# Two attention and token-MLP layers on one core: the weight search moved one block ahead, and PSUM divided once into one-bank tiles

## The chip, the core and the metric

The kernel runs on one core of one Trainium2 chip. A core has a matrix engine (TensorE: PE in the profile, its weight loads PEld), a vector engine (DVE), a scalar engine (ACT), a general engine (POOL), and a queue for DMA issues (SyncE: SP). Matmuls write PSUM, which is divided into eight banks of 128 x 512 fp32 numbers. The metric is the device time of one execution in microseconds (us). The kernel before takes 1268.96 us, the median of three runs from 1268.88 to 1269.1 us.

## The reference

Two layers, each an attention block `A` and an MLP over tokens `B`, with the same weights in both layers. S = 2048 tokens, D = 1024 channels, 32 heads, F = 3584.

```python
def _A_ref(x, wqkv, wo):            # x: (1, 2048, 1024)
    qkv = (x @ wqkv) ...            # 32 heads of 32
    idx = pos[:, None] - arange(8) * 2      # 8 keys, every second token back
    logits = where(idx >= 0, (q . k[idx]) * 32 ** -0.5, -1e9)
    o = softmax(logits) . v[idx]
    return o.reshape(B, S, D) @ wo

def _B_ref(x, w1, b1, w2, b2):
    h = _layernorm(x)
    u = gelu(einsum("bsd,sf->bdf", h, w1) + b1)     # mixes tokens
    return (einsum("bdf,fs->bds", u, w2) + b2).transpose(0, 2, 1)

for _ in range(2):
    x = x + _A_ref(_layernorm(x), wqkv, wo)
    x = x + _B_ref(_layernorm(x), w1, b1, w2, b2)
```

## The kernel before

Tokens are split by parity (`c` = 0, 1: the dilation is 2), so that a query's eight keys are neighbours; each half has eight tiles of 128 tokens. Each layer has these stages in order of time.

1. **Values.** In layer 0 `start_up` normalizes x and multiplies it with the value columns. `V_` (L300) writes a two-bank PSUM tile for each of 16 token tiles, and `E_` (L308, L309) copies both banks to bf16 with one ACT instruction of 128 x 1024. Layer 1 uses `v_proj` with one-bank tiles (L393, L395).
2. **Attention.** 32 visits, two for each of 16 pairs of head group and parity. PE runs per visit: `scores` of this visit (L439), `values` of the visit before (L470 to L487), and two chunks of the query or key projection of the next pair (`qk_chunk`, L408: 8 matmuls each). ACT runs: two copies out of the chunks (L412 or L415), one exponential over a two-bank score tile (L442, 128 x 640), and a logarithm and an exponential for the division (L490, L491). DVE multiplies the exponentials with a band mask (`mask`, L454, four instructions), and divides (L493).
3. **Output projection.** `out_proj`: for each of 16 token tiles two halves of eight matmuls (L523), each followed on DVE by an addition out of PSUM (`add`, L530), and by layer norm pieces (L541, L545, L549) in an order that `chain_` fixes.
4. **First MLP product**, `gemm1`: F is cut into 14 blocks of 256. Block 0 is multiplied plainly (`plain`, L603). Blocks 1 to 13 use a Winograd form of Strassen's scheme: the 2 x 2 blocks of w1 (parity by half of the 256 columns) and of h take 7 products of eight matmuls each (`product`, L700) where a plain product takes 8. I call them P1 to P7, in the order of the code: P1 a(0,0).B11 into `pa`; P2 S0.T0 into `pd`; P3 S1.T1 added to `pb`; P4 a(1,0).B21 added to `pa`; P5 S2.T2 added to `pc`; P6 S3.B22 added to `pb`; P7 a(1,1).T3 added to `pc`; a(c,l) is the part of w1 of parity c and half l of the columns. S0 to S3 are sums of weights (`weight_sum`, DVE, L617), T0 to T3 sums of h (`token_sums`, POOL, L617, made once).
5. **Second MLP product**, `gemm2`: 16 token tiles of two halves, 28 matmuls each (L807), with an addition out of PSUM on DVE (L809).

For P2 to P7 the weights are fp16, and so that no sum overflows, each block of w1 is scaled by a power of two found from its greatest absolute value. That is **the weight search**, in layer 0 alone (layer 1 reads the sums back from DRAM, `load_sums`). For block `far`:

- `top` (L666): two DVE reductions over the two 128 x 2048 weight tiles, one number for each partition;
- `share` (L670, L672): SP writes these 128 x 2 numbers to DRAM (`mxd<-mx`) and, when that has landed, reads them back to all partitions (`bc<-mxd`);
- `power` (L638 to L643): five small DVE instructions make the factor `cs` and its inverse `ci`;
- `scale_w` (L676): ACT scales the two weight tiles, and `weight_sum` makes S0 to S3.

The factors of blocks 1 and 2 are made during attention (`pre_load`, `pre_top`). In block `fb` of the loop the search of `far = fb + 2` stands beside the scaling of `nxt = fb + 1`:

```python
if first and more:
    if nxt > NPRE:
        chain_(V, power, nxt, nxt + 1, bc_[nxt][:])
    chain_(A, scale_w, nxt, 0)
if seek:
    for c in range(DIL):
        chain_(V, top, far, c)
    share(far)
```

Each engine takes its instructions in order. `in_order` fixes the order on PE, and `chain_(V, ...)`, `chain_(A, ...)` that on DVE and ACT. DVE's order in block fb is therefore: power(fb+1), top(fb+2) twice, the addition that makes Y after P5, S0 of block fb+1, the addition that makes Z after P6, S1 to S3 of block fb+1. ACT's order is: `move(pb, pa)` after P1 (L709), `scale_w(fb+1, 0)`, `move(Z, pd)` after P2, `move(pc, pb)` after P3, gelu of `pa`, `scale_w(fb+1, 1)`, three gelus (L715). P5 adds onto what `move(pc, pb)` wrote.

Weights come through a pool of nine tiles of 512 KB (`wp`). A load waits until the tile that it takes over has had its last reader. SP's order is the planner's: it issues the loads of w1 for block fb+4 early in block fb, around the write of that block's sums (`sd<-Sw`, L692), and then the two transfers of `share`.

**PSUM** has three divisions. `psum_pools(m=2, s=2, a=1)` gives two one-bank tiles `m` and three two-bank tiles (`s` twice, `acc`). At the second output tile after the visits, the division becomes eight one-bank tiles `m`, until `gemm1` ends, and then the first one again. Every such switch waits until the tiles of the old division are free.

Of the kernel before, what the change touches and what calls it, by code (L numbers as in the profile page):

```python
# [9 lines left out]
ACT = mybir.ActivationFunctionType  # L10
ALU = mybir.AluOpType
# [6 lines left out]
P = 128  # L18
H = 32
DH = 32  # L20
W = 8
# [7 lines left out]
def kernel(  # L29
# [57 lines left out]
    ps = {}  # L87

    def psum_pools(**bufs):
        if ps:  # L90
            ps.pop("stack").close()
            ps.clear()
        ps["stack"] = ExitStack()
        for n, b in bufs.items():
            ps[n] = ps["stack"].enter_context(tc.tile_pool(name=f"ps{n}", bufs=b, space=bass.MemoryType.PSUM))

    ctx.callback(psum_pools)

    def m_tile():
        return ps["m"].tile([P, 512], FP32, name="m", tag="m")  # L100

    def s_tile():
        return ps["s"].tile([P, 2, 512], FP32, name="s", tag="s")

    def a_tile():
        return ps["a"].tile([P, 2, 512], FP32, name="acc", tag="acc")

    def pair(k):

        k %= 4  # L110
        if k == 3:
            ms = [m_tile(), m_tile()]
            return [m[:] for m in ms], None
        t = a_tile() if k == 1 else s_tile()
        return [t[:, n, :] for n in range(2)], t
# [123 lines left out]
    def start_up(v, wv):  # L239
# [45 lines left out]
        def tr(k, hf):  # L285
            tps[k, hf] = ps["m"].tile([P, KD // 2, P], BF16, name="m", tag="m")
            for j in range(KD // 2):
                lo = (hf * KD // 2 + j) * P
                r = nc.tensor.transpose(tps[k, hf][:, j, :], (xc[k] if k < 2 else xs[k])[:, lo:lo + P], ident[:])
            return r  # L290
# [5 lines left out]
        def V_(k, n, kts):  # L296
            if k not in pss_:
                pss_[k] = a_tile() if k % 3 == 1 else s_tile()
            for kt in kts:
                r = nc.tensor.matmul(pss_[k][:, n, :], lhsT=hT[:, kt, cols(*order[k])], rhs=wv[kt // 2][:, kt % 2, n * 512:(n + 1) * 512],  # L300
                                     start=(kt == 0), stop=(kt == KD - 1))
            return r

        def E_(k):
            c, i = order[k]
            dst, src = v[c][i][:].rearrange("p (n d) -> p n d", n=NDC), pss_[k][:]
            if k < 2:
                return nc.scalar.activation(out=dst, in_=src, func=ACT.Identity, scale=rss[k])  # L308
            return nc.scalar.copy(out=dst, in_=src)  # L309
# [4 lines left out]
        wm = s_tile()  # L314

        def W_(n):
            for _ in range(n):
                r = nc.tensor.matmul(wm[:, 0, :].rearrange("p (n q) -> p n q", q=P), lhsT=warm[:],
                                     rhs=warm[:].unsqueeze(1).to_broadcast([P, 4, P]), start=True, stop=True)
            return r  # L320
# [109 lines left out]
    def scores(u, b):  # L430
        q, k = qB[u % 2], kT[u % 2]
        s0 = (2 * u + b) % NS * HB
        ss = s_tile()
        for i in range(HB):
            lo = (b * HB + i) * P
            for r in range(P // KG):
                rp = slice(r * KG, (r + 1) * KG)
                dst = ss[rp, i // 2, i % 2 * HG * GW:(i % 2 + 1) * HG * GW].rearrange("p (h k) -> p h k", k=GW)
                mm = nc.tensor.matmul(dst, lhsT=k[:, lo + r * KG:lo + (r + 1) * KG],  # L439
                                      rhs=q[:, :, lo + r * KG:lo + r * KG + GW], start=True, stop=True)  # L440
        pc = pcp.tile([P, HB, HG, GW], BF16, name="pc", tag="pc")
        nc.scalar.activation(out=pc[:].rearrange("p (n t) h k -> p n (t h k)", n=2), in_=ss[:, :, 0:2 * HG * GW],  # L442
                             func=ACT.Exp, scale=scale, bias=shift[:])
        exps[:] = pc, s0
        return mm
# [12 lines left out]
    def values(u, b, v, oT):  # L458
        g, c = divmod(u, DIL)
        acc = a_tile()  # L460
# [3 lines left out]
        for i in range(-1 if b else 0, HB):  # L464
            t = t0 + i
            for h in range(HG):
                hp = slice(h * DH, (h + 1) * DH)
                lhs = v[c][t][:, g * P + h * DH:g * P + (h + 1) * DH]
                if i < 0:
                    nc.tensor.matmul(acc[hp, 0, 0:W], lhsT=lhs, rhs=Pm[:, h, sp, P:KW], start=True, stop=False,  # L470
                                     skip_group_check=True)
                else:
                    w = KW if i < HB - 1 else P
                    nc.tensor.matmul(acc[hp, 0, i * P:i * P + w], lhsT=lhs, rhs=Pm[:, h, s0 + i, 0:w],  # L474
                                     start=(t == 0), stop=(i == HB - 1), skip_group_check=True)
        for h in range(HG):
            hp = slice(h * DH, (h + 1) * DH)
            nc.tensor.matmul(acc[hp, 1, :].rearrange("p (t q) -> p t q", q=P), lhsT=ones[:], rhs=Pm[:, h, s0:s0 + HB, 0:P],
                             start=True, stop=False, skip_group_check=True)
# [3 lines left out]
        for lo_, n_, t_ in runs:  # L483
            for h in range(HG):
                hp = slice(h * DH, (h + 1) * DH)
                dst = acc[hp, 1, :].rearrange("p (t q) -> p t q", q=P)[:, t_:t_ + n_, 0:W]
                mm = nc.tensor.matmul(dst, lhsT=ones[:], rhs=Pm[:, h, lo_:lo_ + n_, P:KW], start=False, stop=True,  # L487
                                      skip_group_check=True)
        rd = x2("rd", [P, 512], FP32)
        nc.scalar.activation(out=rd[:], in_=acc[:, 1, :], func=ACT.Ln)  # L490
        nc.scalar.activation(out=rd[:], in_=rd[:], func=ACT.Exp, scale=-1.0)  # L491
        lo = c * SC + t0 * P
        norm.append(lambda: nc.vector.tensor_tensor(out=oT[g][:, lo:lo + HB * P], in0=acc[:, 0, :], in1=rd[:], op=ALU.mult))  # L493
# [99 lines left out]
    def plain(fb, h2, g):  # L593
# [3 lines left out]
        for fl in range(GF):  # L597
            pairs.append([m_tile()[:] for _ in range(NDC)])
# [48 lines left out]
    def gemm1(h2, g, first):  # L647
# [80 lines left out]
        if first:  # L728
            load_w1(2)
            last[A] = normed[0]  # L730
# [7 lines left out]
        load_w1(3)  # L738

        for fb in range(1, NFB):  # L740
            nxt, far = fb + 1, fb + 2
# [3 lines left out]
            pa, pd, pb, pc = (m_tile()[:] for _ in range(4))  # L745
# [8 lines left out]
            if first and more:  # L754
                if nxt > NPRE:
                    chain_(V, power, nxt, nxt + 1, bc_[nxt][:])
                chain_(A, scale_w, nxt, 0)
# [7 lines left out]
            if fb + 3 < NFB:  # L765
                load_w1(fb + 3)
# [8 lines left out]
            if first and more:  # L775
                chain_(V, weight_sum, nc.vector, nxt, 0)
            in_order(product, pb, Ss[fb][:, 3], B22, False)
# [18 lines left out]
    def gemm2(c, i, w2t, g, src, dst, to_hT):  # L796
# [3 lines left out]
        aps, _ = pair(i * DIL + c)  # L800
        parts = [(0, 512, aps[0]), (512, 512, aps[1])]
        final = not to_hT and (c, i) == order[-1]
        if final:
            parts[1:] = [(512, 384, aps[1][:, 0:384]), (896, 128, s_tile()[:, 0, 0:128])]
# [16 lines left out]
    psum_pools(m=2, s=2, a=1)  # L821
    hT, qB = new_hT(), new_qB()
    for li in range(2):
# [77 lines left out]
        for k, (c, i) in enumerate(order[4:]):  # L901
            if k == 1:
                psum_pools(m=8)
# [16 lines left out]
        psum_pools(m=2, s=2, a=1)  # L920
# [39 lines left out]
```

## Time and profile before

| | |
|---|---|
| median of three runs | 1268.96 us |
| the profiled execution, as timed | 1269.96 us |
| its span, first to last instruction | 1268.2 us |
| PE busy | 1233.4 us (97%) |
| DVE / ACT / POOL busy | 565.5 / 484.3 / 75.3 us |
| P1 to P7 of blocks 1 to 13, layer 0 | 275.32 to 449.94 us of the span |
| the same in layer 1 | 913.40 to 1070.53 us |
| one matmul of 128 x 512 after another | 0.216 us |

A row of a timeline has the start and the length in us, the engine, the line, the operation, what it writes and reads, and, where the engine was idle before, for how long and what ended that. PE's matmuls overlap: a row gives 0.38 us for one, but the next begins 0.216 us after it, so that an idle time shown for PE is about 0.16 us shorter than the time lost. Idle time of an engine that is not the bound costs nothing.

### The profile page before, as it was taken

How to read it: one execution, taken by the hardware profiler on the slowest of the kernel's cores; microseconds unless marked ns; L12 is line 12 of the kernel's file. 1: busy time of each engine (PE TensorE's matmuls, PEld its weight loads, DVE VectorE, ACT ScalarE, POOL GpSimd, SP SyncE). 2: the span in 40 equal slices, each digit the busy share in tenths (PEclk: the TensorE clock that was granted, in tenths of full speed). 3: DMA queues.
4: the chain of work that ended last, by engine and by line, in shares of the span. 5: the costliest groups of instructions: out<-in, count | busy, mean ns of one | idle time of the engine just before them, and what ended most of it. 6: DMA issues, size and time to landing. Idle time of an engine off the chain costs nothing.

```text
span 1268.2 us, 19616 instructions
## 1 busy us (share of the span) xinstructions
PE 1233.4 (97%) x8066; PEld 571.8 (45%) x8214; DVE 565.5 (45%) x1073; ACT 484.3 (38%) x755; POOL 75.3 (6%) x79
## 2 busy tenths in 40 slices
PE   9999999999989899999999999999999999999998
PEld 4444444444434444444444444444444444444444
DVE  7467777866676423223210577778411111111111
ACT  5366664476566510000023566645543433000000
POOL 0000000460000000000000000003800000000000
PEclk9999999999999999999999999999999999999999
DMA  8812224755665636457510112246655643335330
GB/s 243 132 50 78 68 83 127 207 161 158 172 179 139 180 87 174 115 133 174 129 50 1 44 50 51 81 168 197 176 153 179 184 143 119 92 108 161 97 94 34
DMA packets 215465, 157.55 MB, mean 124 GB/s; under 512 B 46672, under 2 KB 191824, under 8 KB 212048
## 3 DMA queue, kind: packets, MB, share of 16 engines
q1 hardware_dynamic: 215376, 156.30, 44.6%
q8 instruction: 64, 1.05, 0.4%
q14 instruction: 25, 0.20, 0.1%
HBM read 113.78 MB, written 30.42 MB: 114 GB/s over the span
## 4 chain that ended last, share of the span: by engine, by line
PE 85%; DMA 8%; DVE 5%; issue 1%; ACT 0%; ACTq 0%; SPq 0%
PE m L408 17%; PE s L807 15%; PE m L700 14%; PE m L523 8%; PE acc L807 8%; PE m L807 7%; PE m L393 4%; DMA bc<-mxd 4%; DVE mx L666 4%; PE s L300 3%; DMA mxd<-mx 3%; PE m L603 2%; PE s L439 2%; PE acc L300 1%; PE acc L474 1%
## 5 line engine op out<-in xcount | busy, mean ns | idle before, releaser
L807 PEld LDWEIGHTS <-w 128*128 128x128 bf16 x1820 | 177.0, 98 | 212.2 <-issue 2.3
L408 PE MATMUL m<-hT,wqk 128*128 128x512 bf16 x963 | 223.5, 379 | 6.3 <-issue 4.6
L807 PE MATMUL s<-g,w 128*128 128x512 bf16 (+1 forms) x902 | 199.8, 374 | 2.8 <-ACT g L715 1.7
L700 PE MATMUL m<-T,Sw 128*128 128x512 f16 x624 | 144.7, 382 | 14.3 <-ACT m L709 14.3
L408 PEld LDWEIGHTS <-wqk 128*128 128x128 bf16 x1024 | 95.3, 98 | 117.9 <-issue 10.7
L454 DVE TENSOR_TENSOR Pm<-pc,band 32x640 bf16<-32x640 bf16 x256 | 123.5, 483 | 53.0 <-ACT pc L442 46.4
L700 PEld LDWEIGHTS <-Sw 128*128 128x128 f16 x832 | 81.6, 98 | 115.4 <-issue 19.3
L523 PE MATMUL m<-wo,oT 128*128 128x512 bf16 x500 | 110.9, 379 | 2.9 <-DVE xn L530 2.0
L209 ACT ACTIVATE ln<-mv,eps 128x1 f32<-128x1 f32 x64 | 18.9, 295 | 232.1 <-DVE mv L217 186.2
L807 PE MATMUL acc<-g,w 128*128 128x512 bf16 x442 | 100.3, 379 | 0.4
L700 PE MATMUL m<-h,w 128*128 128x512 bf16 x416 | 98.3, 379 | 0.0
L807 PE MATMUL m<-g,w 128*128 128x512 bf16 (+1 forms) x441 | 97.4, 376 | 0.4
L809 DVE SCALAR_TENSOR_TENSOR xo<-s,b_sb,xs 128x512 bf16<-128x512 f32 (+1 forms) x33 | 24.4, 739 | 161.8 <-PE s L807 135.3
L700 PEld LDWEIGHTS <-w 128*128 128x128 f16 (+1 forms) x624 | 61.0, 98 | 73.6
L617 DVE TENSOR_TENSOR py<-pz,m 128x512 f32<-128x512 f32 x26 | 17.9, 688 | 149.4 <-PE m L700 111.4
L419 DVE COPY qB<-qs 32x512 bf16<-32x512 bf16 x136 | 38.1, 280 | 91.4 <-ACT qs L415 89.9
L523 PEld LDWEIGHTS <-oT 128*128 128x128 bf16 x512 | 49.4, 98 | 62.9 <-DVE xn L530 3.0
L617 POOL TENSOR_TENSOR T<-h 128x512 f16<-128x512 bf16 x16 | 18.5, 1154 | 832.2 <-DMA xr<-xb 581.0
L676 ACT ACTIVATE w<-w,cs 128x2048 f16<-128x2048 bf16 x26 | 51.8, 1998 | 30.1 <-DVE cs L643 30.1
L442 ACT ACTIVATE pc<-s,shift 128x640 bf16<-128x640 f32 x64 | 51.2, 800 | 13.3 <-PE s L439 13.3
L415 ACT CAST qs<-m 128x512 bf16<-128x512 f32 x64 | 37.5, 586 | 48.3 <-PE m L408 48.3
L393 PE MATMUL m<-wv,hT 128*128 128x512 bf16 x251 | 55.2, 379 | 0.3
(95 smaller groups left out, 1187.8 us busy)
## 6 DMA issues: line engine op xcount, KB each, us to landing
w<-in_B_w_dram SPq DMA_DIRECT2D x60, 512.0 KB, 5.8
w<-in_B_w_dram SPq DMA_DIRECT2D x64, 448.0 KB, 4.8
sd<-Sw SPq DMA_DIRECT2D x13, 1024.0 KB, 7.1
Sw<-sd SPq DMA_DIRECT2D x13, 1024.0 KB, 4.9
wqk<-in_A_wqkv_dram SPq DMA_DIRECT2D x16, 512.0 KB, 5.0
xa<-xn SPq DMA_DIRECT2D x32, 256.0 KB, 2.3
xs<-xa SPq DMA_DIRECT2D x32, 256.0 KB, 3.3
wo<-in_A_wo_dram SPq DMA_DIRECT2D x8, 512.0 KB, 5.4
```

The source lines that it names most:

```text
L300: r = nc.tensor.matmul(pss_[k][:, n, :], lhsT=hT[:, kt, cols(*order[k])], rhs=wv[kt // 2][:, kt % 2, n * 512:(n + 1) * 512], start=(kt == ...
L393: nc.tensor.matmul(ps[:], lhsT=hT[:, kt, cols(c, i)], rhs=wv[kt // 2][:, kt % 2, n * 512:(n + 1) * 512], start=(kt == 0), stop=(kt == KD - 1))
L408: mm = nc.tensor.matmul(ps[:], lhsT=wts[part][:, kt, (g % 2) * P:(g % 2 + 1) * P], rhs=hT[:, kt, lo:lo + 512], start=(kt == 0), stop=(kt = ...
L415: nc.scalar.copy(out=qs[:], in_=ps[:])
L419: nc.vector.tensor_copy(out=qB[u % 2][hp, h, ls], in_=qs[hp, :])
L442: nc.scalar.activation(out=pc[:].rearrange("p (n t) h k -> p n (t h k)", n=2), in_=ss[:, :, 0:2 * HG * GW], func=ACT.Exp, scale=scale, bia ...
L454: mm = nc.vector.tensor_tensor(out=Pm[rp, :, s0:s0 + HB, r * KG:r * KG + GW].rearrange("p h t k -> p t h k"), in0=pc[rp], in1=mk, op=ALU.mult)
L523: mm = nc.tensor.matmul(ps[:], lhsT=oT[g][:, cols(c, i)], rhs=wo[n][g // 4][:, g % 4, :], start=(g == 0), stop=(g == NG - 1))
L666: return nc.vector.tensor_reduce(out=bx[fb][:, c:c + 1], in_=w1s[fb][c][:], op=ALU.max, axis=AX.XY, apply_absolute_value=True)
L676: return nc.scalar.activation(out=w[:].bitcast(FP16), in_=w[:], func=ACT.Identity, scale=cs[:, fb:fb + 1])
L700: r = nc.tensor.matmul(out, lhsT=lhs[:, k, :], rhs=rhs[k], start=start and k == 0, stop=stop and k == NI - 1, skip_group_check=True)
L807: nc.tensor.matmul(ap, lhsT=w2t[ft // HF][:, ft % HF, c::DIL], rhs=g[ft // GF][:, ft % GF, lo:lo + w], start=(ft == 0), stop=(ft == FT - 1))
```

## The change

Four edits, in the changed kernel's order:

- **One division of PSUM.** One-bank tiles throughout: two `m`, four `s`, two `a`. Where a two-bank tile stood, `two("s")` or `two("a")` takes two of them. `out_proj` has two `m` where it had eight after its fifth tile. `plain` uses the four `s`; odd blocks of `gemm1` use `a`, `a`, `m`, `m`, even ones the four `s`.
- **Evacuations and exponentials halved.** `E_` has two instructions of 128 x 512 for one of 128 x 1024 (16 times); `scores` has two exponentials of 128 x 320 for one of 128 x 640 (64 times).
- **The search one block further ahead.** `far = fb + 3`; the search of block 3 is made ahead of the loop; w1 is loaded for `fb + 4`, in both layers.
- **`power` moved.** In block fb it makes the factor of block fb+2, and stands on DVE between S0 of block fb+1 and the addition of Z.

```diff
-    def psum_pools(**bufs):
...
+    banks = {n: pool(f"ps{n}", b, space=bass.MemoryType.PSUM) for n, b in (("m", 2), ("s", 4), ("a", 2))}
+    def bank(n):
+        return banks[n].tile([P, 512], FP32, name=n, tag=n)
     def m_tile():
-        return ps["m"].tile([P, 512], FP32, name="m", tag="m")
...
+        return bank("m")
+    def two(n):
+        return [bank(n), bank(n)]
...
         def E_(k):
             c, i = order[k]
-            dst, src = v[c][i][:].rearrange("p (n d) -> p n d", n=NDC), pss_[k][:]
...
+            for n in range(NDC):
+                dst, src = v[c][i][:, n * 512:(n + 1) * 512], pss_[k][n][:]
...
     def scores(u, b):
...
-        ss = s_tile()
+        ss = two("s")
...
-        nc.scalar.activation(out=pc[:].rearrange("p (n t) h k -> p n (t h k)", n=2), in_=ss[:, :, 0:2 * HG * GW],
-                             func=ACT.Exp, scale=scale, bias=shift[:])
+        for n in range(2):
+            nc.scalar.activation(out=pc[:, 2 * n:2 * n + 2].rearrange("p t h k -> p (t h k)"), in_=ss[n][:, 0:2 * HG * GW],
+                                 func=ACT.Exp, scale=scale, bias=shift[:])
...
     def values(u, b, v, oT):
-        acc = a_tile()
+        acc = two("a")
...
     def plain(fb, h2, g):
-            pairs.append([m_tile()[:] for _ in range(NDC)])
+            pairs.append([t[:] for t in two("s")])
...
         plain(0, h2, g)
         if first:
             load_w1(2)
+            load_w1(3)
...
         else:
             chain_(V, scale_a22, 1)
-        load_w1(3)
+            load_w1(3)
+        if first:
+            for c in range(DIL):
+                chain_(V, top, 3, c)
+            share(3)
+        load_w1(4)
         for fb in range(1, NFB):
-            nxt, far = fb + 1, fb + 2
+            nxt, far = fb + 1, fb + 3
...
-            pa, pd, pb, pc = (m_tile()[:] for _ in range(4))
+            pa, pd, pb, pc = (t[:] for t in (two("a") + two("m") if fb % 2 else two("s") + two("s")))
...
             if first and more:
-                if nxt > NPRE:
-                    chain_(V, power, nxt, nxt + 1, bc_[nxt][:])
                 chain_(A, scale_w, nxt, 0)
...
-            if fb + 3 < NFB:
-                load_w1(fb + 3)
+            if fb + 4 < NFB:
+                load_w1(fb + 4)
...
             if first and more:
                 chain_(V, weight_sum, nc.vector, nxt, 0)
+            if first and fb + 2 < NFB:
+                chain_(V, power, fb + 2, fb + 3, bc_[fb + 2][:])
             in_order(product, pb, Ss[fb][:, 3], B22, False)
...
     def gemm2(c, i, w2t, g, src, dst, to_hT):
-        aps, _ = pair(i * DIL + c)
+        aps = [t[:] for t in two("sasm"[(i * DIL + c) % 4])]
...
-    psum_pools(m=2, s=2, a=1)
...
-            if k == 1:
-                psum_pools(m=8)
...
         gemm1(h2, g, first)
-        psum_pools(m=2, s=2, a=1)
```

## The prediction

> **What bounds the kernel now.** I began with the page: PE is busy 97% of the span, and the granted clock is full but for one short stretch. So the time is PE's own work, plus what PE waits for. The view of PE's waits names all of that:
>
> ```profile
> PE m L700 <- ACT m L709: 14.3, 10, 2.3
> PE m L408 <- issue: 4.6, 29, 0.2
> PE m L523 <- DVE xn L530: 2.0, 2, 1.1
> PE s L807 <- ACT g L715: 1.7, 2, 0.9
> ```
>
> The columns are total us, times, longest. Ten waits at L700 make most of it. A table of two stretches shows what they cost: the seven products of blocks 1 to 13 in layer 0 and in layer 1, with the same 716 matmul records.
>
> ```profile
> 275.30:449.90 174.60, 159.61 (x716) 71.44 (x728) 111.25 (x156) 108.41 (x118) 0.68 (x1) 0.99 0.60 164
> 913.40:1070.50 157.10, 156.41 (x716) 71.23 (x728) 22.65 (x38) 64.92 (x94) 0.40 (x1) 1.00 0.53 159
> 296.60:300.00 3.40, 3.24 (x8) 1.14 (x8) 1.49 (x1) 2.70 (x3) 0.00 (x0) 0.50 0.35 85
> ```
>
> Layer 0 takes 17.5 us more. Layer 1 has no wait at L700: a block takes 12.09 us there (twelve blocks from 913.40 to 1058.44). The third row is one short stretch at half clock (0.50), to which I come back. The chain of waits says why layer 0 is slower:
>
> ```profile
> 393.15 3.00 DMA mxd<-mx
> 396.16 0.02 issue
> 396.17 4.68 DMA bc<-mxd
> 400.85 0.02 issue
> 400.87 0.43 DVE m L638
> ...
> 402.06 4.39 DVE mx L666 x2
> ```
>
> This is a loop: search, write, broadcast, `power`, next search. It is closed because `power(fb+1)` stands ahead of `top(fb+2)` on DVE, and its round (4.39 + 3.00 + 4.68, and 1.19 for `power`: 13.3 us) is longer than a block of products. How it reaches PE is in the timeline of one block:
>
> ```profile
> 415.63 2.00 ACT L676 ACTIVATE w<-w,cs 128x2048 f16<-128x2048 bf16 x1 [2.85 <-DVE cs L643]
> ...
> 418.01 0.59 ACT L709 COPY m<-m 128x512 f32<-128x512 f32 x1
> 418.52 0.78 ACT L715 ACTIVATE g<-m,b_sb,ci 128x512 bf16<-128x512 f32 x1
> 418.64 1.89 PE L700 MATMUL m<-T,Sw 128*128 128x512 f16 x8 [1.29 <-ACT m L709]
> ```
>
> `scale_w` waits for the factor, both moves queue behind it, and P5 waits for the second.
>
> **The search, from block 3 on.** With the change, top(fb+3) begins when DVE has made S3 of the block, 1 to 2 us into it, and lasts 4.4; `mxd` and `bc` take 3.0 and 5.1 more (2.8 to 3.3 and 3.9 to 5.5 in the steady blocks' rows), so the broadcast is there 13.5 to 15 us after the block's start, at most 3 us into the next. `power` wants it there only after S0, at about 10.4 us: Y follows P5, `scale_w`'s second half ends at 9.7 by ACT's rows, S0 takes 0.69. So 7 us are spare, and the factor is ready a block before `scale_w` wants it. ACT then runs move (0.57), `scale_w` (2.0), move, move right behind P1 and P3: the last move ends 6.0 us into the block, P5 wants it at 6.9. DVE's sum per block, 4.4 + 1.1 (`power`) + 2 x 0.69 + 4 x 0.69, is 9.7 of 12.09 us. `power` now delays Z and S1 to S3 by 1.1 us; S1 is then ready 0.8 us into the next block and P3 wants it at 3.45.
> On SP, `mxd` and `bc` keep their places and carry the next block's numbers; the loads of w1 keep theirs, in both layers, since nine tiles allow no earlier one. A load issued at a block's start lands 5 to 9 us later, before the next block searches it. So blocks 3 to 13 run at 12.09 us: 132.95 us where they take 449.94 - 303.51 = 146.43. **Gain 13.48.**
>
> **Blocks 1 and 2: where the stall goes.** Here there is no lead yet. These rows are of block 1 and 2 before:
>
> ```profile
> 277.66 4.46 DVE L666 TENSOR_REDUCE mx<-w 128x1 f32<-128x2048 bf16 x2
> 284.21 0.69 DVE L617 TENSOR_TENSOR py<-pz,m 128x512 f32<-128x512 f32 x1 [2.09 <-ACT g L715]
> ...
> 292.53 0.42 DVE L638 TENSOR_REDUCE m<-bc 128x1 f32<-128x256 f32 x1 [4.15 <-DMA bc<-mxd]
> ```
>
> These two reductions were block 3's search inside block 1; now they stand ahead of the loop, at the same time, and block 4's follow. Y of block 1 starts at 277.66 + 2 x 4.39 = 286.44 instead of 284.21, and P7, which may not add to `pc` before Y has read it, at 287.15 instead of 285.68: 1.47 late. Then DVE meets power(3), whose broadcast lands at 292.5 as before (nothing ahead of it on SP has moved). Behind it wait Z, S1, S2, S3. S1 of block 2 is ready at 292.53 + 1.10 + 0.60 + 0.69 = 294.92, and P3 of block 2, due at 290.86 + 1.47 = 292.33, starts at 294.97: 2.64 late. Block 3 then starts at 275.32 + 24.17 + 4.11 = 303.60; before it was 303.51. So nothing is won here, and the question is the clock.
> Before, the longest wait (P5 of block 2 at 296.76, 2.27 by the view, 2.44 lost) is followed by the row at half clock: its eight matmuls take 3.52 us, 1.79 too many. The next longest, 1.79 by the view at 432.68, is followed by full clock. My 2.64 is above the first, so I take the half clock: block 3 at 305.39, **a loss of 1.88**; without it 0.09. If the broadcast comes early enough for S1 in time, the two blocks gain up to 303.51 - 299.49 = 4.02.
> [...]
>
> **One division of PSUM.** The two switches on PE's path go. The wait at L523 is for the switch to eight tiles (223.51 and 861.59, 1.07 and 0.97 by PE's rows); with 0.16 of drain each, 2.36. With two `m` the half that starts there needs only the addition two halves back, done at 221.5. The wait at L807 is the switch back: 2 x (0.87 + 0.16) = 2.06. Now `gemm2` begins in `s`, last used by block 12. **Gain 4.42.**
> What eight tiles covered: a half's addition must now be done before the half after next.
>
> ```profile
> 232.36 0.69 DVE L530 TENSOR_TENSOR xn<-m,xr 128x512 bf16<-128x512 f32 x1 [0.19 <-PE m L523]
> ```
>
> The addition starts 0.2 to 0.3 us after its half and takes 0.69; the bank is wanted 1.73 after. 0.7 us are spare, so zero; if that were gone, each 0.1 us costs 4.4 us over 44 halves. `plain` and the odd and even blocks have the same double buffering as before, at no cost.
>
> **Halves.** Casts of 1024 and 512 (1.003, 0.586 us) give 0.17 fixed and 0.81 ns per element; an exponential (0.80 for 640) then has 0.28 fixed. The next ACT row starts 0.11 before its end, so two halves take 0.86 where one took 0.69: 0.17 more per visit. Cover:
>
> ```profile
> 125.55 0.59 ACT L415 CAST qs<-m 128x512 bf16<-128x512 f32 x1 [0.28 <-PE m L408]
> ```
>
> ACT idles 0.28 before the copy that PE's next chunks need, and the division ends about 0.5 us before `values` wants its bank. So zero; uncovered, 64 x 0.17 = 11 us. The 16 evacuations grow by about 0.1 each (1.6 uncovered), where PE waits for no ACT. A gain is excluded: PE does not wait for either.
>
> **Sum.** 13.48 - 1.88 + 4.42 = 16.0. The span goes from 1268.2 to 1252.2. The profiled execution took 1269.96, the median 1268.96, 0.76 above the span; I keep that: **1252.9 us**; 1251.1 at full clock.
>
> **Rivals.**
> (a) Blocks 1 and 2 run clean, if the first broadcast lands 2.6 us sooner; against it stand 5.0 and 5.3 us for its two transfers behind a 1 MB write. Gain 13.48 + 4.02 + 4.42: 1247.0. Chance 0.06.
> (b) The one division costs: the second exponential or the two banks of `out_proj` reach PE, 4 to 11 us: 1257 to 1264. The spare times above are short but there. 0.07.
> (c) The change does not do what it says: the loop stays closed, through w1's loads instead of `power`. If a load landed 4 us later than the 5 to 9 us of its rows, `top` would wait, and only 4.42 less 1.88 remain: 1266.4. 0.05.
> (d) Slower. `power` stands ahead of Z and S1 to S3 in every block. Were the broadcast over 16 us behind the search's end, in place of 8, every block would stall as block 2 does, 2.64 + 1.79: 11 x 4.43 = 48.7 more than the clean time, so 1252.9 + 48.7 = 1301.6. Spare is 7 us; 0.03.
>
> **Numbers.** My forecast, with and without the half clock, has 0.79. Its bounds are 1251.1 and 1252.9; (a) pulls down, (b) up: 1249.5 to 1257. This kernel's measurement tells about 0.2% from no change. Faster by more: all but (d), and half of (c), 1266.4 being 0.2% below: 0.94. Same 0.03, slower 0.03.
>
> **What would show it.** At L700 no wait for `m` L709; blocks 3 to 13 12.09 us apart; waits of some 1.3 us at P7 of block 1 (for Y) and 2.5 at P3 of block 2 (for S1), then the clock at 0.50 or not; no wait at the first L807 nor at L523; L442 128 times at about 0.53 us; attention's visits still 4.43 us apart. Wrong if the blocks are over 12.2 us apart, if PE waits at L523 for every half, or if `top` waits for a DMA.

## The result, and the profile after

| | before | after |
|---|---|---|
| median, measured together | 1269.03 us (1268.88 to 1269.61, 4 runs) | **1252.58 us** (1252.27 to 1253.94, 4 runs) |
| the profiled execution: timed / span | 1269.96 / 1268.2 us | 1252.65 / 1250.9 us |
| PE busy | 1233.4 us | 1228.8 us |
| ACT busy | 484.3 us | 493.8 us |

The ratio is 0.987 (95% interval 0.985 to 0.989). The forecast was 1252.9 us. The total was nearly exact; some of its terms were not, and one spare time was far off.

Line numbers below are those of the changed kernel unless said otherwise: L685 is the product, L694 the move, L602 the additions and weight sums, L651 `top`, L655 and L657 `share`, L623 the first instruction of `power`, L700 the gelu.

PE's waits after (total us, times, longest):

```profile
PE m L392 <- issue: 4.6, 29, 0.2
PE s L423 <- DMA qB<-qs: 2.6, 2, 1.7
PE s L685 <- ACT s L694: 2.3, 1, 2.3
PE m L685 <- DVE py L602: 1.3, 1, 1.3
```

Ten waits for a move have become one. The two waits in `out_proj` and the two at the start of `gemm2` are gone. The two stretches that the prediction compared, layer 0 and layer 1, with the same columns as there:

```profile
274.60:435.70 161.10, 156.77 (x717) 71.20 (x728) 109.99 (x156) 106.68 (x118) 0.71 (x1) 1.00 0.56 177
897.30:1054.40 157.10, 156.41 (x716) 71.22 (x728) 22.63 (x38) 64.92 (x94) 0.40 (x1) 1.00 0.52 159
```

Layer 0 now takes 4.0 us more than layer 1, where it took 17.5 more. All of the rest lies in blocks 1 and 2, which start 13.55 and 14.60 us before their successors; blocks 3 to 13 take 12.09 each. The timeline of blocks 1 and 2:

```profile
276.99 8.85 DVE L651 TENSOR_REDUCE mx<-w 128x1 f32<-128x2048 bf16 x4
...
285.76 0.67 DVE L602 TENSOR_TENSOR py<-pz,m 128x512 f32<-128x512 f32 x1
...
286.49 1.89 PE L685 MATMUL m<-T,w 128*128 128x512 f16 x8 [1.30 <-DVE py L602]
...
290.36 0.42 DVE L623 TENSOR_REDUCE m<-bc 128x1 f32<-128x256 f32 x1 [3.33 <-DMA bc<-mxd]
...
291.46 0.67 DVE L602 TENSOR_TENSOR pz<-pz,m 128x512 f32<-128x512 f32 x1
...
292.16 0.81 ACT L700 ACTIVATE g<-pz,b_sb,ci 128x512 bf16<-128x512 f32 x1 [4.88 <-DVE pz L602]
292.88 0.76 ACT L700 ACTIVATE g<-m,b_sb,ci 128x512 bf16<-128x512 f32 x1
...
293.54 0.58 ACT L694 COPY s<-s 128x512 f32<-128x512 f32 x1
...
294.18 1.89 PE L685 MATMUL s<-T,Sw 128*128 128x512 f16 x8 [2.35 <-ACT s L694]
```

Both forecast stalls are here. P7 of block 1 waits for Y behind four reductions. P3 of block 2 waits because `power` (290.36) holds Z (291.46); the last step of that chain is ACT's: the gelu of Z, the next gelu and then the move that P3 needs (`COPY s<-s`, 293.54) stand in one queue. No half clock follows:

```profile
294.00:302.80 8.80, 8.57 (x39) 3.90 (x40) 7.14 (x10) 6.38 (x7) 0.00 (x0) 1.00 0.77 254
```

Halved exponentials cost what was worked out, 0.53 us each, and attention's visits are 4.44 us apart (median, by ACT's rows) after as before:

```profile
L427 ACT ACTIVATE pc<-s,shift 128x320 bf16<-128x320 f32 x128 | 60.9, 530 | 13.5 <-PE s L423 13.5
```

The 17.3 us of span, by the starts of the stages in both traces (a wait of x by the view is x + 0.16 lost):

| stretch | gain, us | from |
|---|---|---|
| start to `out_proj`, layer 0 | -0.58 | a wait for `qB` at 185.31 (1.07 lost), not there before; the rest is spread |
| `out_proj` to block 1, layer 0 | 1.24 | the PSUM switch |
| blocks 1 and 2 | 0.04 | two stalls now against one wait (2.44 lost) and a half clock before |
| blocks 3 to 13 | 13.48 | 146.43 to 132.95 |
| last product to `gemm2`, layer 0 | 1.03 | the switch back |
| to `out_proj`, layer 1 | -0.26 | the wait for `qB` there, 1.67 where it was 1.41 |
| `out_proj` to block 1, layer 1 | 1.13 | the PSUM switch |
| last product to `gemm2`, layer 1 | 1.03 | the switch back |
| the end | 0.19 | |

What no view of PE shows is how near the new order is to its limit. These are issues of the changed kernel on SP's queue in one steady block, with the `power` that uses the second broadcast:

```profile
341.76 0.32 SPq L657 DMA_DIRECT2D bc<-mxd  x1
342.18 0.38 SPq L571 DMA_DIRECT2D w<-in_B_w_dram  x1
342.62 0.57 SPq L677 DMA_DIRECT2D sd<-Sw  x1
343.29 1.07 SPq L571 DMA_DIRECT2D w<-in_B_w_dram  x1
345.37 1.90 SPq L655 DMA_DIRECT2D mxd<-mx  x1
...
354.32 0.32 SPq L657 DMA_DIRECT2D bc<-mxd  x1
...
361.57 0.41 DVE L623 TENSOR_REDUCE m<-bc 128x1 f32<-128x256 f32 x1
```

SP waits for the 1 KB of `mxd` to land before it can issue `bc`: 345.37 to 354.32, 8.95 us. Before, these 1 KB took 3.0 us. The DMA issues from 315 to 440 us (KB each, median us to landing) of the kernel before, and then of the changed one:

```profile
sd<-Sw SPq DMA_DIRECT2D x10, 1024.0 KB, 7.2
...
mxd<-mx SPq DMA_DIRECT2D x8, 1.0 KB, 3.0
```

```profile
sd<-Sw SPq DMA_DIRECT2D x10, 1024.0 KB, 8.6
...
mxd<-mx SPq DMA_DIRECT2D x7, 1.0 KB, 8.9
```

The order of the issues is the same; only the time between them changed. These are SP's rows for one block of the kernel before:

```profile
356.88 0.38 SPq L586 DMA_DIRECT2D w<-in_B_w_dram  x1
357.65 0.32 SPq L692 DMA_DIRECT2D sd<-Sw  x1
358.61 0.38 SPq L586 DMA_DIRECT2D w<-in_B_w_dram  x1
366.66 0.32 SPq L670 DMA_DIRECT2D mxd<-mx  x1
369.92 0.32 SPq L672 DMA_DIRECT2D bc<-mxd  x1
```

There `mxd` was issued 8.05 us after the second load, of which 0.30 us were left (it landed at 366.96). Now `mxd` follows 2.08 us after the second load, with the whole 2 MB still under way: that load lands at 353.01 and `mxd` 1.3 us behind it. So SP has become a loop of its own: `bc`, load, sums, load, `mxd`, `bc`. From 329 us on the second load lands 11.1 to 11.4 us after the issue of `bc`, and `mxd` 0.8 to 1.4 us later; the rounds, from one landing of `mxd` to the next, are 12.2 to 12.7 us from 316.68 us on, against 12.09 of a block. The spare time of the broadcast (DVE ready for `power`, less the landing) falls from 4.13 us in block 2 to 0.94 in block 11, and the blocks end just before it is gone.

### The profile page after: what moved, and what is told of

The parts are those of the page before. It is cut to its first block, busy times and chain, and to the rows that moved or that the text cites. A ratio compares the mean times of both kernels' runs of the same rounds, so it can differ in the third digit from the quotient of the medians.

```text
span 1250.9 us, 19776 instructions
## 1 busy us (share of the span) xinstructions
PE 1228.8 (98%) x8066; PEld 571.5 (46%) x8214; DVE 564.2 (45%) x1073; ACT 493.8 (39%) x835; POOL 75.3 (6%) x79
## 4 chain that ended last, share of the span: by engine, by line
PE 94%; DMA 2%; DVE 2%; issue 1%; ACT 1%; SPq 0%; ACTq 0%
PE m L392 17%; PE s L798 16%; PE s L685 11%; PE m L508 9%; PE a L798 8%; PE m L798 8%; PE m L685 7%; PE a L685 5%; PE m L377 4%; PE s L281 3%; PE s L423 2%; PE a L281 1%; PE a L459 1%; PE s L588 1%; PE a L463 1%
## 5 line engine op out<-in xcount | busy, mean ns | idle before, releaser
L798 PE MATMUL s<-g,w 128*128 128x512 bf16 (+1 forms) x906 | 196.8, 374 | 0.9
L685 PEld LDWEIGHTS <-Sw 128*128 128x128 f16 x832 | 81.4, 98 | 100.7 <-DVE Sw L602 1.4
L798 PE MATMUL a<-g,w 128*128 128x512 bf16 x438 | 97.5, 379 | 0.5
L685 PEld LDWEIGHTS <-w 128*128 128x128 f16 (+1 forms) x624 | 61.0, 98 | 75.1 <-issue 1.6
L685 PE MATMUL s<-T,Sw 128*128 128x512 f16 x288 | 66.2, 379 | 2.3 <-ACT s L694 2.3
L602 POOL TENSOR_TENSOR T<-h 128x512 f16<-128x512 bf16 x16 | 18.4, 1153 | 816.1 <-DMA xr<-xb 566.7
L427 ACT ACTIVATE pc<-s,shift 128x320 bf16<-128x320 f32 x128 | 60.9, 530 | 13.5 <-PE s L423 13.5
L396 ACT CAST kT<-m 128x512 bf16<-128x512 f32 x64 | 37.5, 586 | 41.9 <-PE m L392 38.8
L685 PE MATMUL a<-h,w 128*128 128x512 bf16 x224 | 52.9, 379 | 0.0
L685 PE MATMUL m<-T,Sw 128*128 128x512 f16 x224 | 52.9, 379 | 0.0
```

The lines of the kernel that those rows point to most:

```text
L396: nc.scalar.copy(out=kT[u % 2][:, ls], in_=ps[:])
L427: nc.scalar.activation(out=pc[:, 2 * n:2 * n + 2].rearrange("p t h k -> p (t h k)"), in_=ss[n][:, 0:2 * HG * GW], func=ACT.Exp, scale=scal ...
L685: r = nc.tensor.matmul(out, lhsT=lhs[:, k, :], rhs=rhs[k], start=start and k == 0, stop=stop and k == NI - 1, skip_group_check=True)
L798: nc.tensor.matmul(ap, lhsT=w2t[ft // HF][:, ft % HF, c::DIL], rhs=g[ft // GF][:, ft % GF, lo:lo + w], start=(ft == 0), stop=(ft == FT - 1))
```

## The experiments

They ran on three chips, on which the kernel before took 1268.15 (e1 to e4), 1271.07 (e5 to e8) and 1272.03 us (e9 to e11), medians. Ratios are to the kernel before on the same chip.

**e1: the search edits alone**, with the old PSUM and whole exponentials.

```diff
+        if first:
+            for c in range(DIL):
+                chain_(V, top, 3, c)
+            share(3)
...
-            nxt, far = fb + 1, fb + 2
+            nxt, far = fb + 1, fb + 3
...
-                    chain_(V, power, nxt, nxt + 1, bc_[nxt][:])
...
+                chain_(V, power, fb + 2, fb + 3, bc_[fb + 2][:])
```

> The kernel before with the search alone moved (far = fb + 3, power moved, loads one block further); PSUM's three divisions, whole exponentials and whole evacuations stay. My theory: blocks 3 to 13 run 12.09 us apart and win 13.5 us; blocks 1 and 2 lose 1.46 and 2.51 us where they lost 2.44 and, with half clock, 1.79 before; the switches' waits stay (1.0 at the output projection, 0.87 at the second product, in both layers). 1255.3 to 1256.8 us. Rival, that the one-bank tiles carry part of the gain in the blocks: over 1260 us and blocks over 12.2 us apart.

Measured: 1258.03 us (1257.83 to 1258.44), ratio 0.992 (0.991 to 0.993). PE's waits in its trace:

```profile
PE m L700 <- ACT m L709: 2.5, 1, 2.5
PE m L523 <- DVE xn L530: 2.0, 2, 1.1
PE s L813 <- ACT g L715: 1.7, 2, 0.9
```

Blocks 3 to 13 are 12.09 apart, block 2 takes 16.28: the wait of 2.49 at P3 is followed by 3.41 us at half clock. The search edits are most of the gain, and the waits of the PSUM switches stay. The time is 1.2 us above the upper end expected. The trace has what the expectation added up: 13.47 us won in blocks 3 to 13, 1.65 lost in blocks 1 and 2 with the half clock, and a span 12.0 below that of the kernel before. But that span belongs to an execution of 1269.96 us, and the expected range fits a start from the median, 1 us lower; that is most of the miss. All four runs of e1 have a mean clock of 0.999, so the half clock is probably in each, though only one was profiled.

**e2: PSUM and halves alone**, the changed kernel with the search as before (e1's diff reversed).

> The changed kernel with the search as before (far = fb + 2, power ahead of scale_w): one division of PSUM and halved exponentials and evacuations stay. My theory: the four waits for a switch go, 4.4 us, nothing else on the path: 1264.6 us, or up to 1265.9 if the new waits for a query transfer (0.91 us at 185 and 0.26 more at 826 us in the profile after) belong to this part. Rival, that two banks in the output projection or the second exponential cost: 1269 us or more. The ten waits at L700 for the move stay.

Measured: 1264.36 us (1261.56 to 1264.64), ratio 0.9965 (0.995 to 0.998): 3.8 us faster by the medians and 4.4 by the ratio, as expected. Its waits at the products are those of the kernel before:

```profile
PE m L685 <- ACT m L694: 7.2, 5, 1.6
PE s L685 <- ACT s L694: 6.9, 6, 2.2
```

No wait at `gemm2` is left, and none at `out_proj` beyond 0.3 us of issue in all: two `m` banks are enough. By the ratios e1 and e2 together win 10.1 + 4.4 us, 1.7 less than the 16.2 of the whole. e1's half clock would be as much, but each of the three has an interval of over 1.5 us to either side, so the difference is not clear of noise.

**e3: the halves alone**, in the kernel before.

```diff
+            for n in range(NDC):
+                dst, src = v[c][i][:, n * 512:(n + 1) * 512], pss_[k][:, n, :]
...
+        for n in range(2):
+            nc.scalar.activation(out=pc[:, 2 * n:2 * n + 2].rearrange("p t h k -> p (t h k)"), in_=ss[:, n, 0:2 * HG * GW],
+                                 func=ACT.Exp, scale=scale, bias=shift[:])
```

> The kernel before with exponentials and evacuations halved and nothing else changed. My theory: 0.17 us more of ACT per visit lies in ACT's idle time: 1269.0 us, within 0.5, unless the query transfer's wait belongs to it (up to 1270.2). Rival, that the halves are paid: 64 x 0.17 = 11 us, 1280 us.

Measured: 1268.23 us (1266.44 to 1270.5), ratio 1.0003 (0.9994 to 1.0012): free within 1.5 us, where the rival had 11.

**e4: block 3's search earlier**, the changed kernel with top(3) and its `share` ahead of block 1's weight sums on DVE.

```diff
+            for c in range(DIL):
+                chain_(V, top, 3, c)
+            share(3)
             sum_tile(1)
             for n in range(4):
                 chain_(V, weight_sum, nc.vector, 1, n)
...
-        if first:
-            for c in range(DIL):
-                chain_(V, top, 3, c)
-            share(3)
```

> The changed kernel with block 3's search (its two reductions and its two transfers) ahead of the four weight sums of block 1 on DVE, in the 5.1 us in which DVE waits for ACT's scaling. My theory of blocks 1 and 2: the reductions then no longer stand ahead of Y, and the broadcast lands before power(3) is reached, so that the waits of 1.30 and 2.35 us (1.46 and 2.51 lost) both go: 1248.6 us, and no half clock in any run. Rival, that POOL's sums, which run at that time, slow the reductions (the two weight sums beside POOL took 1.32 and 1.53 where others take 0.68), so that S0 of block 1 is late: a wait at P2 of block 1 of 1 us or more, 1250 to 1252 us.

Measured: **1247.85 us** (1247.69 to 1248.39), ratio 0.984 (0.983 to 0.985). No wait in blocks 1 and 2, all thirteen blocks 12.09 apart: both stalls came from the place of block 3's search, as the prediction had it.

**e5: `power` at the end of the block's DVE work.**

```diff
-                chain_(V, power, fb + 2, fb + 3, bc_[fb + 2][:])
...
                 for n in range(1, 4):
                     chain_(V, weight_sum, nc.vector, nxt, n)
+                if fb + 2 < NFB:
+                    chain_(V, power, fb + 2, fb + 3, bc_[fb + 2][:])
```

> The changed kernel, with power(fb+2) moved from its place ahead of Z to behind S1 to S3, at the end of the block's DVE work. Theory: power(3) is what holds Z, and through it ACT's move before P3 of block 2; so the wait of 2.35 us there goes, the wait of 1.30 us of P7 of block 1 for Y stays (Y stands ahead of power in both), and the time is 1252.6 - 2.5 = 1250.1 us (1249.5 to 1250.6). Blocks 3 to 13 stay 12.09 us apart, as the factor is wanted only in the next block's scale_w. Rival: the wait is the broadcast's own, and comes back one step later, at scale_w of block 2 or at P5: 1252 to 1253.

Measured: 1252.53 us (1252.37 to 1252.69), ratio 0.985 (0.984 to 0.987). The wait at P3 of block 2 is gone, as the theory has it, and its 2.5 us are yet not won. (The changed kernel took 1254.06 on this chip, e8, with a half clock in three of four runs; e5 has none.) Waits of PE and, below, of DVE (from 300 to 425 us) in its trace:

```profile
PE s L685 <- DVE py L602: 2.4, 2, 1.5
...
PE m L685 <- DVE py L602: 1.3, 1, 1.3
```

```profile
DVE mx L651 <- DMA w<-in_B_w_dram: 16.4, 10, 3.5
```

Two new waits for Y (372.55 and 397.76) lose 2.7 us, as much as was saved. Y stands behind `top`, and `top` waited ten times for the load of its own weights. PE came into blocks 3 to 13 without the stall of block 2, and the loads, which SP issues behind `bc`, did not come earlier (`bc` for block 6's factor was issued at 317.88 us, in the changed kernel at 316.70). The rival had the time (1252 to 1253) and the kind, a stall that comes back later, and named the place wrongly. This wait of `top` for w1 is the mechanism of the prediction's rival (c).

**e6: exponentials in quarters.**

```diff
-        for n in range(2):
-            nc.scalar.activation(out=pc[:, 2 * n:2 * n + 2].rearrange("p t h k -> p (t h k)"), in_=ss[n][:, 0:2 * HG * GW],
+        for n in range(HB):
+            nc.scalar.activation(out=pc[:, n].rearrange("p h k -> p (h k)"), in_=ss[n // 2][:, n % 2 * HG * GW:(n % 2 + 1) * HG * GW],
```

> The changed kernel, with each visit's exponential in four of 128 x 160 in place of two of 128 x 320. By the terms of the prediction (0.28 us fixed, 0.81 ns an element, next row 0.11 before the end) ACT works 0.34 us longer in each of 64 visits, 21.8 us in all. Theory: this lies beside PE, as the halves did: 1252.6 us, at most 1255 if part of the visits lose a little; attention's visits stay 4.43 us apart. Rival: the halves had used up the cover, and each further us of ACT is paid: up to 1252.6 + 21.8 = 1274 us, visits 4.77 us apart.

Measured: 1254.22 us (1253.62 to 1254.64), beside 1254.06 of the changed kernel on the same chip (e8). The instructions as grouped by form:

```profile
L427 ACT ACTIVATE pc<-s,shift 128x160 bf16<-128x160 f32 x256 | 80.2, 403 | 12.3 <-PE s L423 12.3
```

403 ns for 160 and 530 for 320: 0.28 us fixed and 0.79 ns an element. PE is still not held: the visits are 4.41 us apart (median) in e6 and in e8, and block 1 starts at 273.95 and 274.05 us. So the halves left room. That the two times agree so well is in part chance: e6's trace has a wait of 3.15 us at P3 of block 2 without half clock, and loses 1.5 us in blocks 10 to 12, where the spare time at `power` has run out; e8's has the half clock and loses 0.2.

**e7: the lead without the place.** From block 2 on `power` stands ahead of `top` again, the search stays three blocks ahead.

```diff
+            if first and fb > 1 and fb + 2 < NFB:
+                chain_(V, power, fb + 2, fb + 3, bc_[fb + 2][:])
             if seek:
                 for c in range(DIL):
                     chain_(V, top, far, c)
...
-            if first and fb + 2 < NFB:
+            if first and fb == 1:
                 chain_(V, power, fb + 2, fb + 3, bc_[fb + 2][:])
```

> The changed kernel, with the search three blocks ahead as it is, but from block 2 on power(fb+2) ahead of top(fb+3) on DVE, its place before the change (block 1 keeps the new place). It tells the lead from the place. Theory: the place opens the loop. With power ahead of top, each search again waits for the broadcast of the one before: a round of 4.4 + 3.0 + 4.7 + 1.2 = 13.3 us against 12.09 of a block, now through Y, which stands behind top, so PE waits at P7 for Y in nine or ten blocks (1 to 1.5 us each): 1252.6 + 9.5 x 1.2 = 1264 us (1261 to 1267). Rival: the extra block of lead alone takes the broadcast off the path, since scale_w no longer waits for it: 1252.6 us, blocks 12.09 us apart.

Measured: 1270.32 us (1269.23 to 1271.2), ratio 0.9993 (0.998 to 1.0001): the whole gain is gone, PSUM's with it. PE waits for Y in ten blocks:

```profile
PE m L685 <- DVE py L602: 8.3, 5, 1.9
PE s L685 <- DVE py L602: 7.6, 5, 1.9
PE s L685 <- ACT s L694: 3.0, 1, 3.0
```

Blocks 3 to 10 are 13.65 to 14.12 us apart. So the extra block of lead is worth nothing by itself: the loop opens only with `power` behind `top`. Whether that place would do without the lead no run tests (there `scale_w` of the same block wants the factor). That the time is 6 us above the expected one is the size of the round: here the write takes 3.1, the broadcast 5.4, and `power` with the search 5.6, together 14.1 and not 13.3; and block 2 took 17.76, with a half clock.

**e8: the changed kernel again.**

> The changed kernel itself, once more, beside the three others on the same chip. Theory: 1252.6 us, or 1254.2 where the half clock comes; the wait of 2.35 us at P3 of block 2 and that of 1.30 at P7 of block 1 are the kernel's and recur; the wait of 0.91 us for qB in attention is that execution's and does not. Rival: the wait for qB is the change's and recurs in this profile.

Measured: 1254.06 us (1252.91 to 1255.83), ratio 0.987 (0.985 to 0.988). Both stalls of blocks 1 and 2 recur (1.30 and 2.83), the wait for `qB` in layer 0 does not; it was that one execution's. Two things are new. The wait of 2.83 is followed by half clock; the first row is the stretch with the wait, the second the one at half clock:

```profile
291.86:295.26 3.40, 1.22 (x6) 0.68 (x7) 3.40 (x5) 3.23 (x4) 0.00 (x0) 1.00 0.17 12
295.27:298.67 3.40, 3.40 (x10) 1.22 (x8) 2.91 (x2) 1.69 (x3) 0.00 (x0) 0.50 0.99 255
```

And SP's round is 12.6 to 13.0 us on this chip, so the spare runs out: DVE waits 0.27, 1.30 and 1.35 us at `power` in blocks 9 to 11, and blocks 11 and 12 take 12.16 and 12.21.

**e9: the transfers of `share` on POOL's queue.**

```diff
-            nc.sync.dma_start(out=mxd[fb], in_=bx[fb][:])
+            nc.gpsimd.dma_start(out=mxd[fb], in_=bx[fb][:])
...
-            nc.sync.dma_start(out=bc_[fb][:], in_=mxd[fb].rearrange("p c -> (p c)").partition_broadcast(P))
+            nc.gpsimd.dma_start(out=bc_[fb][:], in_=mxd[fb].rearrange("p c -> (p c)").partition_broadcast(P))
```

> The changed kernel, with the two transfers of share issued from POOL's queue (POOL is idle from 275 us of the span) in place of SP's, so that they stand behind no write of sums and no load of w1. What it tests: in the trace of the changed kernel the write of the search's result lands 7.6 to 9.9 us after its issue in blocks 4 to 11 (3.0 before the change), since the issues of a load, the 1 MB of sums and a load stand ahead of it, and the broadcast's spare time at power falls from 4.1 to 0.9 us over ten blocks; on a second chip it falls below nothing (two waits of 1.3 us at power). Theory: SP's queue is a second loop, of 12.4 to 13.0 us a round against 12.09 of a block. Off that queue, the write lands in 3 to 5 us, the spare is 4 us or more in every block and does not fall, no wait at power after block 1, blocks 3 to 13 12.09 us apart on any chip; the wait at P3 of block 2 shrinks by 0 to 1.5 us: 1251 to 1253 us. Rival: it is the load on the DMA engines themselves, whatever queue: landing times of 8 us stay and the spare falls as before; 1252.6 to 1254.2 us. A third: issues from POOL cost more than SP's, and the blocks are slower, over 1256 us.

Measured: 1257.3 us (1256.61 to 1257.55), ratio 0.988 (0.987 to 0.990). Two effects, of opposite signs. In the steady blocks the theory holds: `mxd` lands in 5.0 us and the sums in 6.4 (medians from 315 to 440 us), the spare at `power` is 4.3 to 9.8 us with no fall, and blocks 3 to 13 are 12.09 apart on a chip where e11 below loses some. But the first `mxd`, issued at 281.02, lands after 6.1 us (4.3 in the trace of the changed kernel), and P3 of block 2 waits twice as long:

```profile
PE s L685 <- ACT s L694: 5.5, 1, 5.5
```

```profile
295.40:298.80 3.40, 2.25 (x6) 0.86 (x6) 3.40 (x4) 3.40 (x4) 0.55 (x1) 0.50 0.42 106
298.82:302.20 3.38, 3.38 (x10) 1.20 (x8) 1.88 (x1) 0.65 (x2) 0.55 (x1) 0.50 1.00 351
```

The half clock lasts 6.83 us here, twice the usual. I had expected a shorter wait at P3, and 1251 to 1253 us. The longer wait has the same source as the gain in the steady blocks: SP no longer stands still until `mxd` has landed. So it issued the load that the changed kernel issues behind this `mxd` (at 281.92) ahead of it (at 277.29); that load landed at 285.81, and `mxd` 1.4 us behind it. The broadcast is there 2.37 us later than in the changed kernel's trace (1.41 of it by `mxd`, the rest by its own issue and landing), and block 2 starts 0.74 earlier: 3.11, the whole difference between the two waits (5.46 and 2.35).

**e10 and e11: block 3's search early, with and without the queue of its own**, on one chip. e11 is e4 again; e10 is e4 with e9's edit from block 4's search on.

> The kernel with block 3's search ahead of block 1's weight sums (1247.85 us in an earlier run, all blocks 12.09 us apart, spare at power from 4.8 down to 0.8 us), with the transfers of share from block 1 on issued from POOL's queue. Theory: no block loses anything with or without it on a chip whose round on SP is 12.4 us: 1247.9 us; where SP's round is 12.9 us the last two blocks would lose some 0.5 us without it and nothing with it. Spare at power 4 us or more in each block. Rival: POOL's issues cost more than they save, 1250 us or more.

> The kernel with block 3's search ahead of block 1's weight sums, once more, beside the two others on the same chip. Theory: 1247.9 us, at most 1249 where SP's round is 12.9 us and its spare runs out in the last blocks; no wait in blocks 1 and 2. Rival: that the first time was one chip's, and the wait at P3 of block 2 comes back: 1251 us or more.

Measured: e10 **1247.94 us** (1247.71 to 1248.13), ratio 0.981 (0.980 to 0.982); e11 1250.26 us (1248.14 to 1251.22), ratio 0.983 (0.981 to 0.984). The write of the search's result from 315 to 440 us, and DVE's waits at `power`, in e11 and then in e10:

```profile
mxd<-mx SPq DMA_DIRECT2D x7, 1.0 KB, 10.2
```

```profile
DVE m L623 <- DMA bc<-mxd: 7.4, 5, 2.5
```

```profile
mxd<-mx POOLq DMA_DIRECT2D x7, 1.0 KB, 5.3
```

In e10 DVE never waits at `power`. e11 loses 2.4 us in blocks 10 to 12 (12.58, 13.41, 12.68), e10 nothing, all thirteen blocks 12.09 apart. e11's expectation put that loss at 1 us at most. SP's mean round is the assumed 12.9 us (from 313.35 us on), but the spare time starts lower than in e8, at 3.9 us, and is gone by block 7 and not in the last blocks. So e10, run on this chip alone, does here what e4 did where SP's round is shorter; both beat the changed kernel.

Spare time at `power` in six traces, in us (below nothing: DVE waits); by the number of the block whose factor is made, from the landing of its broadcast and DVE's row ahead of `power`:

| factor of block | 4 | 6 | 8 | 10 | 12 | 13 |
|---|---|---|---|---|---|---|
| e1, search only | 5.9 | 6.4 | 6.9 | 6.2 | 5.3 | 5.9 |
| after | 4.1 | 3.4 | 2.4 | 1.6 | 0.9 | 0.9 |
| after again (e8) | 5.2 | 3.9 | - | 0.3 | -1.3 | -1.3 |
| e4 | 5.1 | 3.8 | 3.1 | 1.9 | 1.7 | 0.8 |
| e4 again (e11) | 3.9 | 2.2 | 0.4 | -1.0 | -2.5 | -1.8 |
| e10, own queue | 3.7 | 4.3 | 5.9 | 4.2 | 4.8 | 6.1 |

Why e1's does not fall is open. In its trace SP comes to the write of the sums before the sums are made (seven waits, 7.9 us, from 300 to 410 us), where in the changed kernel the write follows at once, and `bc` lands in 4.6 us (median from 315 to 400 us) and not in 5.2. SP waiting for the blocks would hold its round at theirs, and the rounds are 12.1 us on the mean. Its second load is issued 4.0 us (median, at least 3.0) ahead of `mxd`, as in e10 (4.2), where in the changed kernel this lead shrinks from 3.7 to 0.5 us. What keeps SP ahead in e1 no run tests.

## Why the prediction was right, and where not

1. **The loop opened, 13.48 us.** Measured 13.48, and e7 shows that it takes the place of `power`, since the lead alone gains nothing.
2. **"So 7 us are spare": mis-sized.** It took the landing of `mxd` (3.0) from a trace in which all transfers ahead of `mxd` had landed or were about to (at most 1.2 us left in the steady blocks). The text noted that `mxd` and `bc` keep their places on SP, and missed that the search would now end before what stands ahead of them had landed. The write took 8.9, the broadcast was there 20.6 us after the block's start, not 13.5 to 15 (block 6: 339.06 to 359.62), and the least spare was 0.9. In the measured run this cost nothing; in e8 it cost 0.2 us, in e11 2.4. It is rival (d)'s mechanism in small: `power` late, and Z and S1 to S3 behind it. The spare fell by some 0.4 us a block, so that by this estimate a few more blocks would have used it up there too. (DVE's sum per block is 9.64 by the prediction's own terms, not 9.7; nothing rests on it.)
3. **P7 of block 1, 1.47 late for Y:** 1.30 by the view, 1.46 lost.
4. **P3 of block 2, 2.64 late:** 2.35, 2.51 lost. Place and cause were right; the last step was not. I had S1 in time critical at 294.92; the broadcast landed at 290.34 in place of 292.5, S1 was ready at about 292.7, and the move on ACT, behind two gelus of which the first waits for Z, was the last, done at 294.12. I listed what is queued behind `power` on DVE, and not what ACT queues behind Z. So it is luck that the size fits: from the start of block 1, S1 came 1.5 us earlier than reckoned, and the move 1.4 us after S1.
5. **The half clock, 1.79:** taken, and not there in three of four runs. The fourth, with a mean clock of 0.999, took 1253.94, 1.4 more. e8 has it in three of four. Whether it comes is not set by the length of the wait alone: 2.35 us here without it, 2.27 before with it (below).
6. **PSUM, 4.42:** measured 1.24 + 1.13 + 2 x 1.03 = 4.43. Two `m` banks in `out_proj` cost nothing, as the two stretches from its start to block 1 are shorter by just the switch.
7. **Halves, 0:** e3 and e6. Rival (b) is out.
8. **The sum.** The span fell by 17.3 and not 16.0: 1.92 more in blocks 1 and 2 (1.79 of it the half clock that did not come), 0.84 less through two waits for `qB` and the start, 0.2 more at the end and in rounding. The step from span to time was mis-sized the other way: timed runs lie 1.7 above their span, before and after; 0.76 came from setting one execution's span against the median of others. These two errors, 1.3 and 0.95, nearly cancel, and so the closeness of the total is in part luck.

Rival (a), 1247.0, was not the change's time, but it is what the clean blocks 1 and 2 give: 1247.9 in e4 and e10. Rival (c)'s sign, `top` waiting for the load of its weights, is not in the first trace of the changed kernel; it shows for 0.3 us in e8, 1.6 in e6, 2.2 in e11 and 16.4 in e5.

## What to carry to other kernels

Here a landing time went with what was under way when the transfer was issued: the same 1 KB took 2.8 to 3.3 us with at most 1.2 us of the loads left, and 8.9 with 2 MB under way. When a change makes a search end earlier, price its transfer from rows with as much ahead of it, not from those in which everything ahead had landed. When a loop is opened, look for the next one: its round may be longer than the work it hides under (12.2 to 12.7 us against 12.09 here) and still not show, as long as spare time is left over; print that spare time block by block. And where a late instruction holds an engine's queue, follow the wait through the queues of the other engines as well.

## What the runs showed of the hardware

**The half clock: when it came, and behind which waits.** In every trace that has the half clock inside the span's work (before, e1, e7, e8, e9), its record begins 290.13 us after the first record of full clock, and lasts 3.41 us, or 6.83 in e9. Full clock begins 3.7 to 6.8 us after the start of the span, by the run. In the 3.41 us that end where this record begins, PE waited for 2.10 us in the trace before, 2.19 to 2.25 in e1, e7 and e8, and 3.41 in e9. In the trace of the changed kernel the same 3.41 us (290.41 to 293.82 of the span) hold 2.00 us of the wait at P3 of block 2, and no half clock follows. Length alone does not tell: waits of 2.27 (before), 2.49 (e1) and 2.83 us (e8) have half clock behind them and so cost about 1.7 us more (half of 3.41), those of 2.35 (the changed kernel) and 3.15 us (e6) do not. What decides was not shown. While the half clock lasted PE waited for at most 0.24 us in before, e1, e7 and e8, and full clock followed; in e9 it waited for 1.16 us in the first 3.41, and another 3.41 at half clock followed. That is one case.

**The 1 KB of `mxd` landed behind the loads under way, from either queue.** The queue by itself did not set the landing in these traces. `mxd` landed in 10.2 us from SP in e11 and in 5.3 us from POOL in e10 (one chip, medians), but in both less than 1.7 us behind the last load of w1 that had been issued ahead of it (from 315 us on). What differs is when that load was issued: 1.1 us (median) before `mxd` in e11, where SP waits for each `mxd` to land before it goes on, and 4.2 us before it in e10, where it does not. In e1 the load leads by 4.0 us, and `mxd` landed in 5.4 us from SP's own queue. So by these traces what POOL's queue won is that SP need not wait; a run that issued the loads as early from SP's own queue, with the rest as in e10, was not made. With at most 1.2 us of the loads left, as in the kernel before, `mxd` took 2.8 to 3.3 us.

**The same transfers took different times in traces from different chips.** With one trace each, the mean round of SP's queue (from the landing for block 6's factor to that for block 13's) was 12.4 us in e4 and 12.9 in e11, and for the changed kernel 12.5 in its first trace and 12.9 in e8, for the same instructions. The medians of the kernel before, bound by a loop through DMA, went from 1268.15 to 1272.03 us; e4 and e10, in which PE waits for no transfer in the blocks, came to 1247.85 and 1247.94 on the two chips farthest apart.
